# A new TensorE order and a new load order for the opening of a fused attention and feed-forward kernel

## Chip, cores, metric

One core of one Trainium2 chip. The metric is the device time of one execution in microseconds (us).

## The reference, cut

Attention with 8 global and 96 local keys and a bias that grows with the distance, then a feed-forward layer with a squared ReLU. The result is (3072, 512) in fp32.

```python
def _attn_ref(q, k, v, n_global, n_local):           # q, k, v: (4, 8, 768, 64) fp32; 8 global keys, 96 local ones
    scores = (1.0 / np.sqrt(D)) * np.matmul(q, k.transpose(0, 1, 3, 2))
    rel = pos[:, None] - pos[None, :]
    is_global = pos[None, :] < int(n_global)
    is_local = (rel >= 0) & (rel < int(n_local))
    dist = np.where(is_global & ~is_local, float(n_local), np.abs(rel))
    scores = scores + (-slopes[:, None, None] * dist[None, :, :])
    scores = np.where(is_global | is_local, scores, -1000000000.0)
    # ... cut: softmax over the last axis ...
    return np.matmul(a, v)

def _moe_ref(x, w_in, w_out):                        # x: (3072, 512), w_in: (512, 2048), w_out: (2048, 512)
    h = np.maximum(x @ w_in, 0.0)
    return h * h @ w_out
```

## The kernel before

The kernel holds q, k, v and the weights in fp16. A class `Plan` receives all work as operations with needs and estimated costs, and lists it. The order on TensorE and the order of the loads (issued by GpSimd) are given; the orders on ScalarE and VectorE, and which of the eight PSUM banks a product takes, follow from the plan's own simulation. So a new TensorE order moves VectorE's and ScalarE's work too.

For the first batch the TensorE order is one string. T2 turns q and k of tile 2 (a tile is 128 tokens; T0 turns two tiles). S2o and S2b are scores of tile 2 against its own keys and against those of the tile before. V2 is not TensorE work: VectorE copies v of tile 2 to `vb` and puts the global rows of tile 0 into it. A20 and A21 multiply by v (four heads each), X20 and X21 turn the result for the first layer, and F, G, E, D are first-layer blocks of tile 0, tiles 1 and 2, tiles 3 and 4, and tile 5. F0, G00 and G01 need quarter c0 of w_in, F1 and G10 need c1, and so on.

```python
OPENING = """T0 T2 S0o S1b A01 S1o A00 T3 S2b X01 S2o A10 A11 T4 S3b V1 X00 X11 A21 S4o A20 F1 X21 S3o
X10 S4b X20 F0 G00 V2 T5 V3 V4 G11 A30 G10 A31 S5o G30 G31 S5b A41 G01 F3 X30 G21 A40 X31 F2
X40 X41 G20 A50 E00 A51 E01 E11 X50 X51 E10 D0 D1"""
    # ... cut ...
LOADING = """v0 k2 q2 k3 v2 v1 q3 v4 k4 q4 c1 c0 q5 k5 v3 c3 v5 c2"""
```

How a name of the load string becomes a DMA, and what V and A need:

```python
        def rows(src, name, t, rank=None):
            def emit(e):
                dst = (x.bt.v[:, x.half * HT + t, :, 0:D] if name == "v"
                       else staged(x, name)[:, t, :, :])
                dma = nc.gpsimd.dma_start(out=dst, in_=src[x.b, :, r0 + t * P:r0 + (t + 1) * P, :]
                                          .rearrange("h p d -> p h d"))
                if x.hb > 3 and name == "sq" and t == 0:
                    for turn in halves[x.hb - 1].turns + halves[x.hb - 2].turns[-1:]:
                        behind(dma, turn)
                if name == "sk":
                    x.last_load = dma
            return plan.load(0.86, emit, vbefore if name == "v" else before, rank,
                             1.6 if x.hb == 0 else 2.6)
    # ... cut ...
    def load_w_in(c):
        n = d_ff // 4
        w_in_op[c] = plan.load(2.55, lambda e: nc.gpsimd.dma_start(
            out=w_in_sb[:, :, c * n:(c + 1) * n],
            in_=moe_w_in[:, c * n:(c + 1) * n].rearrange("(k p) f -> p k f", p=P)))
    # ... cut ...
    def fix_v(bt, t0, t1):
        def emit(e):
            copy(e, bt.vb[:, t0 - 1:t1 - 1], bt.v[:, t0:t1])
            copy(e, bt.vb[0:GR, t0 - 1:t1 - 1], bt.v[0:GR, 0:1].to_broadcast(
                [GR, t1 - t0, H, D + 1]))
        op = plan.add({"DVE": 0.85}, emit, [bt.v_in[0], *bt.v_in[t0:t1]],
                      wait=0.0 if bt is batches[0] else 4.0)
        for t in range(t0, t1):
            bt.vb_ops[t] = op
    # ... cut ...
        needs = st["weighs"][a0 // 2::2] + [bt.v_in[r]]
        if r > 0:
            needs.append(bt.vb_ops[r - 1] if r > 1 else bt.v_in[0])
        job = plan.pe(4 * len(kinds) * 0.035, emit, needs, 1)
    # ... cut ...
    for name in LOADING.split():
        load_jobs[name]()
    # ... cut ...
    for name in OPENING.split():
        jobs[name]()
```

Where the plan expects TensorE to stand still ahead of a product that takes a bank, and only before 24 us, it puts in products with a tile of zeros ("dummies"), to hold the clock:

```python
    def warm(ps):
        fp32 = ps.dtype == FP32
        n = min(512, ps.shape[-1]) if fp32 else P
        for _ in range(int(plan.spare / (n / 2400 + 0.003))):
            if fp32:
                nc.tensor.matmul(ps[:, 0:n], lhsT=zero[:, 0:P], rhs=zero[:, 0:n], start=True,
                                 stop=True)
            else:
                nc.tensor.transpose(out=ps[:, 0:n], in_=zero[:, 0:P], identity=ident)
```

The softmax here doesn't subtract the row's maximum and nothing guards it: scores larger than these inputs give would overflow.

## Time and profile before

| | before |
|---|---|
| time, median of 3 | 214.99 us (214.2 to 215.36) |
| time, median of 6, beside the changed kernel | 214.40 us (214.2 to 215.36) |
| span in the trace | 212.7 us |
| start of S0o, the first product after T2 | 9.95 us |
| start of D0, the last block of the opening | 37.89 us |
| from S0o to D0 | 27.94 us |

All that the change can touch lies before D0. From there both kernels run the same work with TensorE never idle, so **the start of D0 is the marker**: read it first, and ask what moved it. In the TensorE timeline it is found 0.87 us (one block of eight products) after the start of the line that ends the opening. The prediction below shows the page and the timelines of this kernel. One view it only tells of is VectorE's timeline (start, length, engine, line, operation, output and input, shape, count; in brackets idle time ahead and what ended it):

```profile
12.42 0.91 DVE L202 COPY vb<-v 128x520 f16<-128x520 f16 x2
13.25 0.16 DVE L770 RECIPROCAL rec<-av 128x4 f32<-128x4 f32 x1
```

A V is two copies of 0.7 to 0.9 us together, and each A's norm is a reciprocal and a product (0.55 from start to start). They stand in one queue: a late V makes every norm behind it late, and X needs the norm.

### The profile page before, as it was taken

The page shows a single profiled execution, that of the slowest core. Times are in us where ns is not written, and L with a number is a line of the kernel's source. Part 1 is how long each engine was busy: PE and PEld are TensorE (multiplying, and loading weights), DVE is VectorE, ACT ScalarE, POOL GpSimd, SP SyncE. Part 2 cuts the span into 40 slices and gives each one's busy share as a digit, 9 for nine tenths or more (in the row PEclk, how much of TensorE's full clock was granted, in tenths as well). Part 3 has the DMA queues.
Part 4 walks back from the last instruction along what each step waited for, and adds up shares of the span by engine and source line. Part 5 has one row for each costly group of instructions (what it writes and reads, how often), then busy time and mean ns, then how long its engine had stood idle before and what let it go on. Part 6 is the DMA issues. An engine that isn't in the chain of part 4 may idle for free.

```text
span 212.7 us, 4804 instructions
## 1 busy us (share of the span) xinstructions
PE 206.0 (97%) x1908; PEld 127.3 (60%) x1908; DVE 116.7 (55%) x334; ACT 122.0 (57%) x250; POOL 66.6 (31%) x82
## 2 busy tenths in 40 slices
PE   6799999999999999999999999999999999999994
PEld 7587889755464565456654665456644665456553
DVE  7598987443582579409770679219860777114300
ACT  6789985644741885148821994148811994237421
POOL 8994643694000940095006800094000000000000
PEclk9999999999999999999999999999999999999999
DMA  6999999999935999599976997299952100320012
GB/s 176 166 174 188 191 207 210 161 154 163 201 120 154 107 154 154 133 118 172 148 113 119 158 135 146 73 137 177 130 121 99 52 18 19 89 99 2 0 52 99
DMA packets 106343, 27.06 MB, mean 127 GB/s; under 512 B 96976, under 2 KB 103376, under 8 KB 106320
## 3 DMA queue, kind: packets, MB, share of 16 engines
q0 software_dynamic: 74944, 13.11, 80.2%
q1 hardware_dynamic: 30320, 13.11, 26.7%
q10 hardware_dynamic: 1056, 0.52, 0.8%
q8 instruction: 15, 0.25, 0.5%
q14 instruction: 8, 0.07, 0.1%
HBM read 27.26 MB, written 6.29 MB: 158 GB/s over the span
## 4 chain that ended last, share of the span: by engine, by line
PE 93%; DMA 3%; POOL 1%; DVE 1%; ACT 0%; issue 0%; POOLq 0%
PE hps L560 40%; PE yps L609 37%; PE sp L464 4%; PE av L519 4%; DMA sq<-in_q_dram 3%; PE yps L637 2%; PE sp L721 2%; PE av L760 1%; PE sp L714 1%; PE trp L669 1%; PE trx L787 1%; PE trp L411 1%; POOL v L312 0%; POOL sk L312 0%; DVE tm L772 0%; ACT qk L200 0%
## 5 line engine op out<-in xcount | busy, mean ns | idle before, releaser
L560 PE MATMUL hps<-xt,w_in_sb 128*128 128x384 f16 (+2 forms) x608 | 88.5, 301 | 0.0
L609 PE MATMUL yps<-w_out_sb,h 128*128 128x512 f16 x368 | 83.0, 379 | 0.0
L560 PEld LDWEIGHTS <-w_in_sb 128*128 128x128 f16 x608 | 53.8, 98 | 26.6
L584 ACT ACTIVATE hr<-hps 128x384 f16<-128x384 f32 (+1 forms) x106 | 54.9, 526 | 14.4 <-PE hps L560 13.3
L609 PEld LDWEIGHTS <-h 128*128 128x128 f16 x368 | 34.9, 98 | 39.0
L200 ACT COPY y<-yps 128x512 f32<-128x512 f32 (+1 forms) x25 | 14.2, 569 | 66.4 <-PE yps L609 63.8
L595 DVE TENSOR_TENSOR h<-hr 128x768 f16<-128x768 f16 (+1 forms) x70 | 35.5, 519 | 23.2 <-ACT hr L584 22.8
L312 POOL DMA_DIRECT2D sq<-in_q_dram x22 | 19.4, 889 | 66.0 <-DMA xt<-tm 64.3
L477 ACT ACTIVATE ex<-sp 128x512 f16<-128x512 f32 x66 | 35.0, 621 | 1.2 <-PE sp L464 1.2
L586 DVE TENSOR_SCALAR hr<-hps 128x384 f16<-128x384 f32 (+1 forms) x16 | 9.0, 562 | 39.4 <-PE hps L560 39.4
L312 POOL DMA_DIRECT2D v<-in_v_dram x24 | 21.7, 926 | 4.4 <-DMA w_out_sb<-in_moe_w_out_dram 3.7
L497 DVE TENSOR_TENSOR phat<-ex,mask 128x1024 f16<-128x1024 f16 (+1 forms) x36 | 20.2, 596 | 2.4 <-ACT ex L477 2.4
L312 POOL DMA_DIRECT2D sk<-in_k_dram x22 | 19.5, 901 | 5.0 <-DMA w_out_sb<-in_moe_w_out_dram 3.1
L529 DVE TENSOR_TENSOR tm<-av,rec 128x384 f16<-128x384 f32 x24 | 13.4, 557 | 0.8
L519 PEld LDWEIGHTS <-phat 128*128 128x128 f16 x240 | 9.8, 97 | 3.1
L519 PE MATMUL av<-v,phat 128*128 128x65 f16 x144 | 10.9, 193 | 0.0
L202 DVE COPY vb<-v 128x520 f16<-128x520 f16 (+1 forms) x32 | 9.9, 309 | 1.6 <-DMA v<-in_v_dram 0.9
L519 PE MATMUL av<-vb,phat 128*128 128x65 f16 x96 | 10.1, 194 | 0.0
L202 DVE COPY kb<-qk 128x96 f16<-128x96 f16 (+4 forms) x56 | 8.1, 203 | 2.0 <-ACT qk L200 2.0
L464 PEld LDWEIGHTS <-qk 64*128 64x128 f16 x168 | 6.3, 94 | 4.6 <-issue 3.7
L464 PE MATMUL sp<-qk 64*128 64x128 f16 x168 | 8.8, 218 | 0.0
L527 DVE RECIPROCAL rec<-av 128x6 f32<-128x6 f32 x24 | 4.7, 194 | 7.0 <-PE av L519 6.6
(66 smaller groups left out, 136.6 us busy)
## 6 DMA issues: line engine op xcount, KB each, us to landing
out_dram<-y SPq DMA_DIRECT2D x23, 256.0 KB, 2.2
v<-in_v_dram POOLq DMA_DIRECT2D x24, 128.0 KB, 6.5
sk<-in_k_dram POOLq DMA_DIRECT2D x22, 128.0 KB, 6.2
sq<-in_q_dram POOLq DMA_DIRECT2D x22, 128.0 KB, 5.6
w_in_sb<-in_moe_w_in_dram POOLq DMA_DIRECT2D x4, 512.0 KB, 10.1
w_out_sb<-in_moe_w_out_dram POOLq DMA_DIRECT2D x4, 512.0 KB, 14.1
y<-in_k_dram ACTq DMA_DIRECT2D x2, 256.0 KB, 4.9
y<-in_q_dram SPq DMA_DIRECT2D x2, 256.0 KB, 4.4
```

Source lines behind the costliest of these rows:

```text
L200: nc.scalar.copy(out=out, in_=in_)
L202: eng(e).tensor_copy(out=out, in_=in_)
L312: dma = nc.gpsimd.dma_start(out=dst, in_=src[x.b, :, r0 + t * P:r0 + (t + 1) * P, :] .rearrange("h p d -> p h d"))
L464: nc.tensor.matmul(sp[h][:, i, :], lhsT=lhsT, rhs=bt.qk[rows, 0, r, a, :], start=True, stop=True)
L477: nc.scalar.activation(out=st["ex"][:, h], in_=sp[h], func=AF.Exp, scale=scale)
L497: eng(e).tensor_tensor(out=x.phat[a][:, :, t0:t0 + n], op=ALU.mult, in0=st["ex"][:, :, i0:i0 + 2 * n].rearrange("p e (t b) c -> p e t (b c ...
L519: nc.tensor.matmul(av[:, h, j, :], lhsT=lhsT, rhs=rhs, start=not before, stop=before or r == 0)
L529: nc.vector.tensor_tensor(out=st["tm"].rearrange("p t e d -> p e t d"), in0=av[:, :, :, 0:D], in1=rec[:, :, :, None].to_broadcast([P, 2, H ...
L560: nc.tensor.matmul(st["ps"][:, i * n:(i + 1) * n], lhsT=w_in_sb[:, kk, m * P:(m + 1) * P], rhs=x.xt[:, kk, c0:c1], start=kk == 0, stop=kk ...
L584: nc.scalar.activation(out=o, in_=i, func=AF.Relu)
L595: eng(e).tensor_tensor(out=x.h2[:, m0:m0 + width, c0:c1], in0=hr, in1=hr, op=ALU.mult)
L609: nc.tensor.matmul(st["ps"], lhsT=x.h2[:, m, j * P:(j + 1) * P], rhs=w_out_sb[:, m, :], start=m == 0, stop=m == NFT - 1)
```

## The change

The intent: an order found by a search, which counts with eight shared banks, and with a load as done only when the last of its DMA engines has landed. Nothing else is touched.

```diff
--- before.py
+++ after.py
@@ -17,13 +17,13 @@
 
 
 
-OPENING = """T0 T2 S0o S1b A01 S1o A00 T3 S2b X01 S2o A10 A11 T4 S3b V1 X00 X11 A21 S4o A20 F1 X21 S3o
-X10 S4b X20 F0 G00 V2 T5 V3 V4 G11 A30 G10 A31 S5o G30 G31 S5b A41 G01 F3 X30 G21 A40 X31 F2
-X40 X41 G20 A50 E00 A51 E01 E11 X50 X51 E10 D0 D1"""
-
-
-
-LOADING = """v0 k2 q2 k3 v2 v1 q3 v4 k4 q4 c1 c0 q5 k5 v3 c3 v5 c2"""
+OPENING = """T0 T2 S0o S1o S2b V1 S1b A00 T3 V2 A01 S2o A10 S3o A11 A21 T4 X11 X01 S3b A20 X00 T5 X21 S4o
+X20 X10 F1 S4b A31 G11 V3 G10 G01 F0 A41 X31 A30 G00 S5b A40 F3 X30 G30 F2 X41 V4 X40 S5o
+G21 E10 E00 E11 A50 G20 A51 X50 G31 X51 E01 D0 D1"""
+
+
+
+LOADING = """v1 q2 k2 k3 q3 v0 v2 q5 q4 k4 k5 c1 v3 c0 v4 c3 c2 v5"""
```

Of the order, S1o, S2b and S1b now stand ahead of the first A, and V1 and V2 early. Of the loads, v1 goes first and v0 sixth, all of q and k ahead of the weights.

## The prediction

> **What bounds the kernel now.** I read first the page's shares and the chain that ended last, then the busy time by stretch, then the TensorE timeline of the first 46 us with its waits, and last the VectorE and ScalarE timelines there.
>
> ```profile
> PE 206.0 (97%) x1908; PEld 127.3 (60%) x1908; DVE 116.7 (55%) x334; ACT 122.0 (57%) x250; POOL 66.6 (31%) x82
> ...
> PE 93%; DMA 3%; POOL 1%; DVE 1%; ACT 0%; issue 0%; POOLq 0%
> ```
>
> TensorE is busy 206.0 of 212.7 us and holds 93% of the chain. By stretch (columns: window, length, then busy us and count of PE, PEld, DVE, ACT, POOL):
>
> ```profile
> 5.00:10.00 5.00, 3.45 (x49) 2.90 (x47) 3.31 (x7) 3.97 (x9) 5.00 (x7) 1.00 2.26 179
> ...
> 15.00:20.00 5.00, 4.56 (x96) 3.74 (x93) 4.04 (x17) 4.83 (x12) 3.10 (x4) 1.00 1.42 197
> 20.00:25.00 5.00, 5.00 (x76) 4.26 (x73) 4.58 (x14) 5.00 (x13) 2.89 (x4) 1.00 1.86 183
> ...
> 50.00:100.00 50.00, 50.00 (x452) 28.14 (x450) 28.91 (x88) 28.63 (x59) 16.00 (x19) 1.00 1.28 147
> ```
>
> From 20 to 200 us TensorE never stops, so nothing can be won there by order. The change touches only what runs before about 38 us, and the question is how early the opening's list is worked off. The marker is the first 128-column product of D0, which both lists put last: in the timeline it comes 0.87 us (one E block) after the start of the last line below, so at 37.89 us.
>
> ```profile
> 7.56 0.89 PE L216 MATMUL trp<-ident,zero 128*128 128x128 f16 x13
> 9.49 0.40 PE L669 MATMUL trp<-ident,sq 128*128 128x128 f16 x4 [1.04 <-DMA sq<-in_q_dram]
> ...
> 11.70 0.62 PE L213 MATMUL av<-zero 128*128 128x260 f16 x4
> ...
> 13.29 0.33 PE L216 MATMUL trp<-ident,zero 128*128 128x128 f16 x3
> ...
> 17.83 0.20 PE L760 MATMUL av<-vb,ph 128*128 128x65 f16 x1
> 18.42 0.40 PE L721 MATMUL sp<-qk 64*128 64x128 f16 x8 [0.40 <-ACT qk L200]
> ...
> 37.02 8.02 PE L560 MATMUL hps<-xt,w_in_sb 128*128 128x256 f16 x72
> ```
>
> T2 starts at 9.49, when its q tile lands. The products with "zero" are dummies that the kernel puts into expected waits, so they count as lost time and not as work.
>
> **How much is lost in the opening.** I add up the real work after T2's start from the distances between starts in this timeline: T 0.45 (4 of them), S with the distance products 0.87 (5), S without 0.33 and 0.10 of pause ahead of it (6), A of row 0 0.13 (2), other A 0.25 (10), X 0.11 (12), F 0.89 (4), G and E 0.87 (12). That is 1.80 + 4.35 + 2.58 + 0.26 + 2.50 + 1.32 + 3.56 + 10.44 = 26.8 us. The stretch lasts 37.89 - 9.49 = 28.4 us. So about 1.6 us are lost: 0.46 and 0.17 in dummies, some 0.7 around A21 and S4o (16.7 to 18.4 us), about 0.15 before T5 at 23.05, the rest in small pieces. **1.6 us, 0.75% of the time, is the most that a better order after T2 can win**; another 1.9 us lie before T2, from 7.56 to 9.49.
>
> **What the Trainium skill says.**
> - "DMA: Bandwidth & Descriptors", section "Why a DMA increments its semaphore by 16 and not by 1": a transfer runs on up to 16 engines and only the full 16 means that all data landed. That is the "last landing" which the search counts. The trace gives one landing per load, and it is what ends the wait: the third load, q2, is issued at 3.60 and lands 5.8 us later; T2 starts at 9.49.
> - "PSUM — Partial Sum Buffer", section "PSUM bank collisions raise a hardware error": two engines must not touch one bank at once, and a compiler serialises ScalarE against VectorE too. The trace agrees: T2's result is copied by ScalarE at 10.15 for 0.59 us and by VectorE only at 10.77. So a tile turned by both engines costs the sum of both copies.
> - "TensorE: Matmul & The Clock Gate", section "Part 1: The HAM clock gate": the clock falls after some 3.4 us of idleness, and warm 128-column products start 55.6 ns apart. Here 8 transposes take 0.45 us, 56 ns each, and the granted clock is 1.00 in every stretch. The longest gap in the new order is far shorter, so the dummies that it drops should not cost clock.
>
> **The change part by part.**
> *Dummies.* The instruction order of the built kernels has 40, 13, 4 and 3 dummies before, 40, 13 and 1 after. That takes out three wide ones at about 0.11 us and three narrow ones at 0.056: 0.5 us of TensorE time, which counts only if no wait comes in its place.
>
> *Loads.* The same 18 loads in another order. They land at a steady pace: in the order before, the issue plus the time to landing gives 7.7, 8.5, 9.45, 10.3, 11.3, 12.25, 13.0, 14.1, 15.4, 15.9 us for the ten small ones, then c1 18.3, c0 20.8, q5 21.6, k5 22.8, v3 23.8, c3 25.9, v5 26.9, c2 29.3; so about 0.95 for a small one, 2.4 for a w_in quarter. I keep the pace and deal the new names out. q2 is second (8.5), k2 third (9.45): the q half of T2 can run early and only 4 transposes remain after 9.49, so T2 ends 0.23 us earlier. v0 goes from first to sixth (7.7 to 12.25). q5 and k5 come before the weights (14.1, 16.8), c1 moves to 19.2, c0 to 22.7, c3 stays at 25.8, c2 to 28.3.
>
> *The order.* The new list does five score blocks at once after T2 (two waves of eight banks) and puts A, X and F behind. I walk it with these rows: an exp 0.49 from start to start (four take 2.06, the last 0.60), a qk copy 0.34 on VectorE or 0.49 on ScalarE, reciprocal and tm 0.55 a pair, V 0.70 to 0.83, kb 0.5, two mask products 0.75, an X copy 0.24.
>   - TensorE runs S0o S1o S2b S1b A00 T3 A01 S2o without a stop from 9.72 to 14.78. ScalarE follows with the exps: S0o at 10.7, S1b's second ends at 14.9. A10 waits for it, 0.15.
>   - VectorE is the tight one. V1 needs v0, so it starts at 12.35. In its order stand V1, V2, A00's norm, two T3 copies (both on VectorE now), A01's norm, kb, A10's and A11's norm: 0.80 + 0.70 + 0.55 + 0.68 + 0.55 + 0.5 + 0.55 + 0.55 = 4.9, plus 0.08 for the end of the last: 17.3. X11 needs A11's norm; TensorE is done with T4 at 16.75. **Stall 0.6.** A21 waits 0.15 for S2o's exps on the way.
>   - VectorE goes on: A21's norm, S3o's two mask products, X01's copy, A20's norm (19.4), kb, T5's copy (20.2), after which ScalarE copies T5's other half in the same bank, to 20.85. X20 waits about 0.1 for A20's norm, S4b waits 0.25 for T5.
>   - From S4b (20.9) on I find no further stop. G01 at 23.2 has c0 at 22.7; F0 ends at 25.0 and A41's weights are ready at 24.9; F3 at 27.2 has c3 at 25.8; F2 at 29.0 has c2 at 28.3.
>
> Losses after: 0.15 + 0.15 + 0.6 + 0.1 + 0.25, some 1.3 us, of which 0.23 is eaten from the earlier end of T2. So D0 starts at 9.49 - 0.23 + 26.8 + 1.3 = 37.4, against 37.9: **0.5 us earlier**. As TensorE is without a pause from there to the end, the 0.5 goes through whole: 214.99 - 0.5 = 214.5. Since my VectorE durations are somewhat long (V and kb were slower where GpSimd issued next to them), I lean by 0.1: 214.4 us.
>
> **The rivals.**
> 1. *The search's own hope*: all waits gone, the whole 1.6 us plus 0.2 from T2: 213.2. For it: VectorE needs only to be 0.5 faster than in my walk for X11 to start on time. Against it: VectorE would work without a pause from 12.3 to 20, which no stretch of the profile before shows (4.58 of 5 us at most).
> 2. *The chain of v0*: the move of v0 from first to sixth makes V1, V2 and all norms late, and the stall at X11 and those behind it (X20, S4b, A41) grow instead of sharing one delay. Each 0.1 us of extra VectorE time is then on the path. For it: the walk shows VectorE and ScalarE (exps and relus without a gap until 24.5) both full. That makes 215 to 215.8.
> 3. *A load lands late*: c0, c2, k4 have only 0.5 to 0.9 us of slack; two w_in quarters swapped with small ones could shift landings by 1 us. Plus 0.5 to 1: about 215.2.
> 4. *The gain is lost later*, in the phase after 45 us. The profile speaks against it: TensorE waits for nothing there, and the w_out quarters land by about 39.5 while their first use is at 44.88.
>
> **Range and chances.** Rival 1 and rival 2 lie about evenly about the estimate; the three times before span 1.2 us. 8 in 10: 213.5 to 215.3. Faster by 2% would need 4.3 us, more than all that is lost after 7.56; slower by 2% would need several new stalls or a late load of 4 us. So within 2%: 0.97, faster 0.01, slower 0.02.
>
> **What would show it right or wrong.** Right: T2's q transposes stand before 9 us and its k ones at about 9.5; the wait list of TensorE names VectorE's tm before an X block near 17 us with 0.4 to 0.8; VectorE is busy almost without a pause from 12.3 to 20; D0 begins at 37.2 to 37.6; TensorE is full from 25 us on. Wrong: a wait of TensorE on a DMA after T2 (rival 3), D0 after 37.9 (rival 2), no wait above 0.2 after 10 us and D0 by 36.5 (rival 1), or a difference in the total that D0's start does not show (rival 4).

## More of the kernel before

`V1` is two copies: the first reads only v1, the second only v0.

## The result, and the profile after

| | before | after |
|---|---|---|
| median of 6 | 214.40 us (214.2 to 215.36) | 213.82 us (213.74 to 213.89) |
| ratio | 1 | 0.9963 (95%: 0.9943 to 0.9982) |
| span in the trace | 212.7 | 212.0 |
| S0o starts | 9.95 | 9.35 |
| D0 starts | 37.89 | 37.12 |
| S0o to D0 | 27.94 | 27.77 |

A ratio here is the mean time of one kernel's fast runs over that of the other's of the same rounds, so not quite the ratio of the medians. The gain is real (the interval excludes 1) and small: 0.6 us of the median, 0.77 us at D0. Against 2% it counts as the same.

The page of the changed kernel, engine shares and the chain that ended last:

```profile
PE 206.4 (97%) x1902; PEld 127.6 (60%) x1902; DVE 116.3 (55%) x332; ACT 122.5 (58%) x252; POOL 66.5 (31%) x82
...
PE 88%; POOL 6%; DMA 5%; DVE 0%; ACT 0%; issue 0%; POOLq 0%
```

TensorE has six products fewer (the dummies). The chain looks different: GpSimd and a DMA now hold 11% instead of 4%. Its pieces in order of time (start, length, what) tell which:

```profile
9.75 1.75 POOL sk L312 x2
13.07 9.78 DMA w_in_sb<-in_moe_w_in_dram
22.90 1.94 PE hps L560 x24
```

GpSimd issues load after load without a pause until 13.07, where it issues c0; c0 lands at 22.9, and G01, its first user, starts on that. In the kernel before the same view went from q2's landing straight over into TensorE's work.

The busy time by stretch (columns as in the prediction: window, length, busy us and count of PE, PEld, DVE, ACT, POOL, then clock, DMA share, GB/s):

```profile
5.00:10.00 5.00, 4.60 (x60) 4.32 (x59) 3.47 (x6) 4.42 (x10) 5.00 (x7) 1.00 2.26 179
...
15.00:20.00 5.00, 4.73 (x90) 3.68 (x87) 4.61 (x19) 4.64 (x11) 3.46 (x5) 1.00 1.50 196
20.00:25.00 5.00, 4.90 (x73) 4.16 (x71) 4.48 (x15) 4.68 (x11) 2.33 (x4) 1.00 1.47 198
```

TensorE is busy 1.15 us longer ahead of 10 and 0.17 longer between 15 and 20, and 0.10 shorter between 20 and 25, where it was full before. Busy is not the same as won: about 0.5 of the 1.15 us is T0, whose 16 transposes started 107 ns apart in this trace (5.89 to 7.60) and about 60 in the other, with waits between them. The granted clock reads 1.00 in both and doesn't show this. T0 ends close to 7.6 us in both and T2's k half waits for a load after it, so nothing is lost or won by it. The TensorE timeline at the places that the prediction named:

```profile
8.32 0.39 PE L669 MATMUL trp<-ident,sq 128*128 128x128 f16 x4
9.11 0.40 PE L669 MATMUL trp<-ident,sk 128*128 128x128 f16 x4 [0.40 <-DMA sk<-in_k_dram]
9.35 0.61 PE L714 MATMUL sp<-dmask,slope_id 128*128 128x128 f16 x8
...
16.42 0.40 PE L669 MATMUL trp<-ident,sk 128*128 128x128 f16 x4
16.86 0.40 PE L787 MATMUL trx<-ident,tm 128*128 128x128 f16 x4
...
36.25 8.02 PE L560 MATMUL hps<-xt,w_in_sb 128*128 128x256 f16 x72
```

T2 runs in two halves, at 8.32 and 9.11. X11 starts at 16.86. D0 follows the last line by 0.87, at 37.12.

Short waits are hidden in this timeline, because the ends of pipelined products are modelled and overlap the next ones. The waits of the weight loads show them. The wait list of PEld from 9 to 40 us (total, times, longest):

```profile
PEld L669 <- DMA sk<-in_k_dram: 0.8, 2, 0.6
PEld L787 <- DVE tm L772: 0.5, 2, 0.3
PEld L560 <- DMA w_in_sb<-in_moe_w_in_dram: 0.4, 1, 0.4
```

In words: T2 and T4 wait for their k tiles, X11 and X20 for VectorE's `tm`, and G01 for c0:

```profile
22.89 1.77 PEld L560 LDWEIGHTS <-w_in_sb 128*128 128x128 f16 x24 [0.38 <-DMA w_in_sb<-in_moe_w_in_dram]
```

VectorE's timeline, to set beside the lines of before:

```profile
10.90 0.72 DVE L202 COPY vb<-v 128x520 f16<-128x520 f16 x1
11.98 0.39 DVE L202 COPY vb<-v 32x520 f16<-32x520 f16 x1 [0.35 <-DMA v<-in_v_dram]
12.94 0.63 DVE L202 COPY vb<-v 128x520 f16<-128x520 f16 x2 [0.58 <-DMA v<-in_v_dram]
13.50 0.16 DVE L770 RECIPROCAL rec<-av 128x4 f32<-128x4 f32 x1
```

V1's big copy runs at 10.90, long before v0 lands; only its small second copy waits for v0. V2 waits for v2 and is done just ahead of the first norm.

### The profile page after: what moved, and what is told of

It is laid out like the page before. It is cut to its first block, busy times and chain, and to the rows that moved or that the text cites. A ratio compares the mean times of both kernels' runs of the same rounds, so it can differ in the third digit from the quotient of the medians.

```text
span 212.0 us, 4795 instructions
## 1 busy us (share of the span) xinstructions
PE 206.4 (97%) x1902; PEld 127.6 (60%) x1902; DVE 116.3 (55%) x332; ACT 122.5 (58%) x252; POOL 66.5 (31%) x82
## 4 chain that ended last, share of the span: by engine, by line
PE 88%; POOL 6%; DMA 5%; DVE 0%; ACT 0%; issue 0%; POOLq 0%
PE hps L560 39%; PE yps L609 38%; DMA w_in_sb<-in_moe_w_in_dram 5%; PE sp L464 4%; PE av L519 4%; POOL v L312 2%; POOL sk L312 2%; POOL sq L312 2%; PE yps L637 2%; PE trp L411 1%; PE av L760 1%; POOL w_in_sb L369 0%; PE trx L787 0%; PE sp L721 0%; DVE ident L239 0%; ACT y L200 0%
## 5 line engine op out<-in xcount | busy, mean ns | idle before, releaser
L586 DVE TENSOR_SCALAR hr<-hps 128x384 f16<-128x384 f32 x15 | 8.3, 554 | 38.7 <-PE hps L560 38.7
```

## The experiments

The theory after the trace, called A in the texts: the opening is set by whatever wait ends last, and that is c0's landing or VectorE's queue; a shift at D0 passes whole into the time. B is the rival that each text names. Times stand beside runs of the kernel before in the same rounds on the same chip. Edits are to the changed kernel unless it says otherwise.

### 1. The loads alone

```diff
-LOADING = """v0 k2 q2 k3 v2 v1 q3 v4 k4 q4 c1 c0 q5 k5 v3 c3 v5 c2"""     (order of the kernel before kept)
+LOADING = """v1 q2 k2 k3 q3 v0 v2 q5 q4 k4 k5 c1 v3 c0 v4 c3 c2 v5"""
```

> The order of before with the new order of loads. Theory A (order and loads only work together): F0 in the old order stands at 21.15 us and now needs c0, which lands at 22.9 in the trace of after instead of 20.8; TensorE waits about 1.7 us there, the wait of T5 (0.14) goes, everything behind F0 follows unchanged, so D0 starts about 39.5 instead of 37.9 and the time is about 216.0 us, 0.7% above before. Theory B (the gain comes from the loads, because T2's q half runs early): at or below 213.9.

Measured: 216.0 us beside 214.38, ratio 1.0075 (1.0062 to 1.0088). **The new loads alone cost 1.6 us.** The old order asks for c0 early, with F0; it lands later now, and the plan filled the wait with dummies. TensorE's timeline:

```profile
21.64 1.03 PE L213 MATMUL hps<-zero 128*128 128x512 f16 x4
22.78 1.39 PE L560 MATMUL hps<-xt,w_in_sb 128*128 128x128 f16 x19
```

F0 stands at 22.78, 1.6 us behind the 21.15 of the kernel before. D0 starts at 39.39, 1.5 later.

### 2. The order alone

```diff
-OPENING = """T0 T2 S0o S1b A01 S1o A00 T3 S2b X01 ...        (loads of the kernel before kept)
+OPENING = """T0 T2 S0o S1o S2b V1 S1b A00 T3 V2 A01 ...
```

> The order of after with the old order of loads. Theory A (order and loads only work together): T5 stands at 17.9 us in the new order and k5 lands at 22.8 in the old order of loads, so TensorE stops for 4 to 5 us at T5, of which the 0.3 at c0 and some small waits come back: about 218 us, 1.7% above before. Theory B (the gain comes from the TensorE order, with fewer dummies): at or below 213.9.

Measured: 217.88 us beside 214.38, ratio 1.0164 (1.015 to 1.0178). **The new order alone costs 3.5 us.** It asks for T5 early, and the old loads bring q5 and k5 behind two quarters of weights:

```profile
18.81 3.79 PE L216 MATMUL trp<-ident,zero 128*128 128x128 f16 x65
22.44 0.39 PE L669 MATMUL trp<-ident,sq 128*128 128x128 f16 x4
```

The 65 dummies fill 3.6 us in front of T5. So neither half carries the gain: each alone loses more than both together win.

### 3. c0 later by one load

```diff
-... c1 v3 c0 v4 c3 c2 v5
+... c1 v3 v4 c0 c3 c2 v5
```

> After, with the load of v4 put ahead of c0. Theory A (the landing of c0 at 22.9 us is what the end hangs on in after, all earlier waits being slack): c0 lands one small load later, 0.9 us, and the time rises by 0.8 to 0.9, to about 214.7 us. Theory B (the VectorE chain from v0 binds, as my prediction had it, with c0 0.5 us ahead of its need): 0.4 or less.

Measured: 214.37 us beside 214.38, ratio 0.9997 (0.9985 to 1.001); the changed kernel's was 0.9963.

```profile
23.61 1.10 PE L560 MATMUL hps<-xt,w_in_sb 128*128 128x256 f16 x9 [0.76 <-DMA w_in_sb<-in_moe_w_in_dram]
...
36.95 1.26 PE L560 MATMUL hps<-xt,w_in_sb 128*128 128x256 f16 x12
```

c0 lands at 23.57 instead of 22.85. G01 starts 0.72 us later than in the changed kernel, D0 0.70 later (37.82, 0.87 after the last line), the median 0.55. From c0's first use to D0 it is 14.21 us here (37.82 - 23.61) and 14.23 there (37.12 - 22.89). A delay of c0 passes through whole: **c0's landing is on the path**, with no slack. The time itself lies between the numbers of the two theories and would not decide between them; the equal shifts of G01 and D0 do.

### 4. k4 earlier

```diff
-... v2 q5 q4 k4 k5 c1 ...
+... v2 q4 k4 q5 k5 c1 ...
```

> After, with q4 k4 loaded ahead of q5 k5; the same instructions on TensorE. T4's wait for k4 (about 0.25 us at 16.2) should vanish. Theory A (c0 binds): no change of the time, within 0.1 us of 213.8, while the wait at G01 for c0 grows by what T4 saves. Theory B (the waits from 15 to 20 us are on the path): 0.2 us less.

Measured: 213.8 us beside 214.38, ratio 0.9974 (0.996 to 0.9987): no change. T4 no longer waits for k4, but X11 starts where it did:

```profile
16.09 0.39 PE L669 MATMUL trp<-ident,sk 128*128 128x128 f16 x4
16.84 0.40 PE L787 MATMUL trx<-ident,tm 128*128 128x128 f16 x4 [0.36 <-DVE tm L772]
```

The wait for k4 turned into a longer wait for `tm`. Up to X11, VectorE's queue is the limit, and the two waits lay beside each other. A's number came, but not its detail: the wait at G01 did not grow (its weight loads waited 0.25 us, against 0.38 in the changed kernel).

### 5. The kernel before without its late dummies

```diff
     def warm(ps):
+        plan.warmed = getattr(plan, "warmed", 0) + 1      (the kernel before)
+        if plan.warmed > 2:
+            return
```

> Before, without the seven dummy products after T2 (four wide ones ahead of A01, three narrow ones ahead of T3). Theory A: they stand in waits that stay (A01 waits for ScalarE's exps, T3 for the landing of q3), so taking them out gives at most 0.15 us: 214.3. Theory B (dropping dummies is TensorE time won, 0.63 us, and explains the gain of after): 213.8.

Measured: 214.44 us beside 214.44, ratio 0.9999 (0.9987 to 1.0012). The time is A's, but its reason is not what the trace shows. S0o starts at 9.99, 0.04 later than before, yet S4o 0.24 earlier (18.18 instead of 18.42), and T5 0.23 earlier. Then TensorE's weight loads for G30 wait for c3:

```profile
18.18 0.40 PE L724 MATMUL sp<-qk 64*128 64x128 f16 x8 [0.16 <-ACT qk L200]
26.10 1.64 PEld L563 LDWEIGHTS <-w_in_sb 128*128 128x128 f16 x16 [0.29 <-DMA w_in_sb<-in_moe_w_in_dram]
```

(The first line is from TensorE's timeline, the second from that of its weight loads.) c3 lands at 26.06; in the kernel before, TensorE came to G30 at 26.16. So some 0.28 of the dummies' 0.63 us was TensorE time in the way, and leaving them out won it as far as G30, where the old order of loads took all but 0.06 back. Leaving them out costs no clock: T5's products still start 55 ns apart. Whether the six that the change drops are a part of its gain, this run can't say.

### 6. A30 ahead of G01, to cover the wait for c0

```diff
-... V3 G10 G01 F0 A41 X31 A30 G00 ...
+... V3 G10 A30 G01 F0 A41 X31 G00 ...
```

> After, with A30 moved from behind X31 to ahead of G01, the first user of c0. Theory A (c0's landing at 22.8 to 22.9 us is what the end hangs on): the wait of 0.27 us at G01 is filled with A30's 0.25 us of work, all behind G01 is shorter by that, 213.6 us. Theory B (the path runs elsewhere, the wait at G01 is only its shadow): no change, 213.8.

Measured: 213.88 us beside 214.44, ratio 0.997 (0.9958 to 0.9983): the same as the changed kernel, where A had expected a gain. G01 does not wait for c0 any more, but G10 ends at 22.97 instead of about 22.64, so with A30's 0.25 TensorE comes to G01 at 23.21. The reason stands on VectorE:

```profile
12.94 1.08 DVE L200 COPY vb<-v 128x520 f16<-128x520 f16 x2 [0.56 <-DMA v<-in_v_dram]
13.95 0.16 DVE L768 RECIPROCAL rec<-av 128x4 f32<-128x4 f32 x1
```

V2's two copies took 1.08 us against 0.63 in the changed kernel (about 0.85 in runs 3 and 4), so the first norm came 0.45 us later and X11 stood at 17.19. The wait was not removed; VectorE's queue had become the limit.

### 7. T2's loads first, with A30 ahead

```diff
-LOADING = """v1 q2 k2 k3 q3 v0 v2 q5 q4 k4 k5 c1 v3 c0 v4 c3 c2 v5"""     (and the edit of 6)
+LOADING = """q2 k2 k3 q3 v0 v2 v1 q4 k4 q5 k5 c1 v3 c0 v4 c3 c2 v5"""
```

> As the run with A30 ahead, and the loads in the order q2 k2 k3 q3 v0 v2 v1 q4 k4 q5 k5, then as in after: k2 lands at about 8.1 instead of 9.1, so T2 and what follows it starts about 0.8 us earlier, and v0 and v2 land a place earlier. c0 keeps its place. Theory A (c0 caps): the time is that of the run with A30 ahead, within 0.1 us, and the wait at G01 grows to 0.5 us or more. Theory B (the start at T2 and the VectorE chain are the path): 0.5 us or more below it, about 213.1.

Measured: 213.95 us beside 214.44, ratio 0.9976 (0.9963 to 0.9988): no gain. T2 is done earlier (its second half starts at 8.84), but the plan put two dummies behind it and S0o starts at 9.50. And v1 is now seventh, so both V come late and in one piece:

```profile
12.09 1.83 DVE L200 COPY vb<-v 128x520 f16<-128x520 f16 x4 [0.85 <-DMA v<-in_v_dram]
```

The first norm follows at 13.85, and X11 stands at 17.24. A had the time right, but not the reason: it saw c0, and the limiter was VectorE's queue.

### 8. An order and loads of my own search

```diff
-OPENING = """T0 T2 S0o S1o S2b V1 S1b A00 T3 V2 ...       (and warm as in 5)
+OPENING = """T0 T2 S0o S2b S2o V1 A00 S1b X00 A01 V2 S1o T3 A21 S3b ...
-LOADING = """v1 q2 k2 k3 q3 v0 v2 q5 q4 k4 k5 c1 v3 c0 v4 c3 c2 v5"""
+LOADING = """k2 q2 v0 v1 q3 k3 v2 q4 k4 k5 q5 c1 c0 v3 v4 c3 c2 v5"""
```

> An order of TensorE and loads of my own, with T2's loads first and c0 ahead of v3, v4 (so c0 lands about 21.9), no dummies after T2. If the loads of the weights and the start at T2 are what binds, freeing both gives 0.4 to 0.8 us below after, 213.0 to 213.4. If the waits of VectorE and ScalarE take over (the order was chosen with rough durations), it gives nothing or loses: 213.8 or more.

Measured: 216.26 us beside 214.44, ratio 1.008 (1.0067 to 1.0094): slower. The order was chosen with rough durations. TensorE's wait list from 9 to 40 us:

```profile
PE trx L790 <- DVE tm L775: 1.7, 3, 1.1
PE av L763 <- ACT ph L737: 0.8, 2, 0.6
PE sp L724 <- DVE qk L202: 0.7, 2, 0.4
```

That is 3.2 us of waits for VectorE and ScalarE. A search over an order is worth what its durations are worth.

### 9. V2 held back

If VectorE's queue ahead of X11 is the limit, take V2 out of it. V2 was held until behind A21's norm, and `warm` was cut as in 5:

```diff
     op = plan.add({"DVE": 0.85}, emit, [bt.v_in[0], *bt.v_in[t0:t1]],
-                  wait=0.0 if bt is batches[0] else 4.0)
+                  wait=(5.0 if t0 == 2 else 0.0) if bt is batches[0] else 4.0)
```

> After, with V2 (two VectorE copies, 0.63 to 1.08 us in the traces so far, first needed by A31) held back behind A21's norm, so that A00's to A11's norms come that much earlier; no dummies after T2. Theory A (two limits of nearly the same length: c0's landing at 22.85 us and the VectorE chain through V2): X11 starts before 16.75 us, but G01 then waits longer for c0, and the time stays at 213.7 to 213.8. Theory B (the VectorE chain alone binds): 213.4 or less.

Measured: 214.43 us beside 214.43, ratio 0.9995 (0.9982 to 1.0009): the whole gain lost. Both theories missed. VectorE's timeline:

```profile
13.16 0.18 DVE L771 RECIPROCAL rec<-av 128x4 f32<-128x4 f32 x1 [0.67 <-PE av L761]
...
17.50 1.00 DVE L200 COPY vb<-v 128x520 f16<-128x520 f16 x2
```

and TensorE's at X20:

```profile
20.04 0.40 PE L788 MATMUL trx<-ident,tm 128*128 128x128 f16 x4 [0.94 <-DVE tm L773]
```

Without V2, VectorE idles 0.67 us ahead of the first norm. V2's full microsecond stands at 17.50 instead, ahead of S3o's masks and A20's norm, and X20 waits 0.94 us. The first norm comes 0.34 us sooner than in the changed kernel (13.16 against 13.50), but X11 does not (16.84 against 16.86), because T4 still waits for k4, until 16.61. VectorE's norm after X11 stands at 17.16 against 17.18, so up to there V2 had cost the changed kernel nothing. **VectorE is a queue of work and not one late wait**: what is moved out of one place is paid at the next.

### 10 and 11. The same with A30 ahead, and with k4 early too

```diff
+ the edit of 6, on that of 9                (10)
+ the edits of 6 and 4, on that of 9         (11)
```

> As the run with V2 held back, and A30 ahead of G01. Theory A (two limits; the run with A30 ahead alone gained nothing because V2 took 1.08 us there): now both are eased, and 0.25 us is won, 213.5 to 213.6; c2's landing at 28.4 is the next limit and lets no more through. Theory B (c0's wait is no limit): as the run with V2 held back.

> As the run before, with q4 k4 ahead of q5 k5 in the loads, so that T4 doesn't wait for k4. Theory A: no more than that run, within 0.1 us, as c0 and c2 stay where they are; theory B (the stretch from 15 to 18 us is on the path): 0.2 us less.

Measured: 214.34 us (0.9993, 0.9979 to 1.0007) and 214.16 us (0.9983, 0.9969 to 0.9997), beside 214.43. The first loses nearly all of the gain, the second about half of it. The second's six times fall into two groups, 213.86 to 214.0 and 214.31 to 214.49; its trace is from the slower one, and what divides them is not known. X20 waits 0.95 and 0.91 us again. S0o starts at 9.21 in the first and at 9.55 in the second, yet D0 at 37.65 and 37.69. That is no clean test of an early start, since k4 moved too: the chain that ended last goes back to k4's landing at 16.41 in the first, and to k2's at 9.27 in the second.

### 12. The v tiles ahead, with A30 ahead

Here V1 and V2 are to be done before the first norm needs VectorE.

```diff
-LOADING = """v1 q2 k2 k3 q3 v0 v2 q5 q4 k4 k5 c1 v3 c0 v4 c3 c2 v5"""     (and the edit of 6)
+LOADING = """v1 q2 k2 v0 v2 k3 q3 q4 k4 q5 k5 c1 v3 c0 v4 c3 c2 v5"""
-                  wait=0.0 if bt is batches[0] else 4.0)
+                  wait=(1.2 if t0 == 1 else 0.0) if bt is batches[0] else 4.0)
```

> As the run with A30 ahead, but V2 taken off the VectorE chain without putting it on another stretch: v0 and v2 are loaded ahead of k3 and q3, k4 ahead of q5, and VectorE does V1 and V2 before A00's norm is ready (13.2 us) instead of after. Theory A (two limits, VectorE's queue of work up to 20 us and c0's landing at 22.85): X11 starts by 16.7 us instead of 16.86 to 17.2, TensorE reaches G01 with A30 done at about 22.6 to 22.8 and waits for c0 up to 0.3 us; the time is 213.5 to 213.6, 0.25 us below after, and no lower, as c0 and c2 stay. Theory B (something behind G01 binds): 213.8.

Measured: 213.7 us (213.46 to 213.77) beside 214.49, ratio 0.9959 (0.9946 to 0.9972), not to be told from the changed kernel's 0.9963. VectorE:

```profile
12.56 1.01 DVE L200 COPY vb<-v 128x520 f16<-128x520 f16 x2
13.49 0.16 DVE L768 RECIPROCAL rec<-av 128x4 f32<-128x4 f32 x1
```

V2 is early, but takes 1.01 us, and the first norm stands at 13.49, as in the changed kernel (13.50). G01 starts at 22.97 without a wait. Then F2 finds the next landing, that of c2:

```profile
28.69 0.90 PEld L558 LDWEIGHTS <-w_in_sb 128*128 128x128 f16 x16 [0.29 <-DMA w_in_sb<-in_moe_w_in_dram]
```

D0 starts at 37.12, to the hundredth where it does in the changed kernel.

### The runs side by side

| run | S0o | D0 | S0o to D0 | median beside before | wait that the trace shows as the limit |
|---|---|---|---|---|---|
| before | 9.95 | 37.89 | 27.94 | | S4o for ScalarE's `qk` |
| after | 9.35 | 37.12 | 27.77 | -0.58 | G01 for c0 |
| 1 | 9.46 | 39.39 | 29.93 | +1.62 | F0 for c0 |
| 3 | 9.29 | 37.82 | 28.53 | -0.01 | G01 for c0 |
| 4 | 9.26 | 37.06 | 27.80 | -0.58 | X11 for `tm`, then G01 for c0 |
| 5 | 9.99 | 37.83 | 27.84 | 0.00 | G30 for c3 |
| 6 | 9.43 | 37.17 | 27.74 | -0.56 | X11 for `tm` |
| 7 | 9.50 | 37.21 | 27.71 | -0.49 | X11 for `tm` |
| 9 | 9.30 | 37.79 | 28.49 | 0.00 | X20 for `tm` |
| 12 | 9.39 | 37.12 | 27.73 | -0.79 | F2 for c2 |

D0 tells the time within 0.25 us in each row (columns 3 and 5, against before). Five kernels (after, 4, 6, 7, 12) end within 0.15 us of each other at D0, by three different waits. No version clearly beats the changed kernel. Runs 2, 8, 10 and 11 are left out of the table; their times stand above.

## Why the prediction was right, point by point

- **The bound was right.** Only the time before D0 moved, and it passed through: 0.77 us at D0, 0.7 in the span, 0.6 in the median. From 25 us on TensorE is full. The search's own hope (213.2, all waits gone) and the slow rivals (about 215 and more) were not what came; the estimate of 214.4 was 0.6 too high, because it started from the median of three runs, 214.99, and the six runs give 214.40. The gain itself, estimated at 0.5 (0.6 with the lean), was 0.58 in the medians.
- **Its own signs came only in part.** T2's q half ran before 9 us, and TensorE was full from 25 us on. D0 at 37.12 fell just outside 37.2 to 37.6, the waits for `tm` before X11 and X20 were 0.3 at most and not 0.4 to 0.8, and VectorE still idled 0.58 us ahead of V2. One sign of "wrong" came too, TensorE's waits for loads after T2 (k4, c0), though not the 0.5 to 1 us that rival 3 gave them.
- **T2's two halves were right in kind.** The q half ran before 9 us, at 8.32. The k half came at 9.11 and not at 9.5, since the third load landed about 0.35 us sooner than the pace of before had it. With the same first three loads, T2's k half started between 8.97 and 9.32 in nine kernels' traces; with the old first three, T2 started at 9.15 to 9.54 in three. So this difference is of the size of the spread, and I cannot say that the order of the loads made it.
- **How much of the gain is S0o's earlier start is not shown.** It is 0.60 us earlier, the time from S0o to D0 only 0.17 shorter; the prediction had 0.23 and 0.3, so that its sum came near is in part luck. Against booking 0.60 to T2: in the changed kernel D0 is pinned by c0's landing (run 3), and the chain leads from there to GpSimd's issues and not to T2. For it: in the five kernels that end alike the time from S0o to D0 is 27.71 to 27.80 us, while S0o starts anywhere from 9.26 to 9.50. No run moved k2's landing alone with the rest of the changed kernel kept.
- **The stall of X11 was mis-sized.** I had 0.6 us, the trace shows about 0.2. The step that failed is "V1 needs v0, so it starts at 12.35": only V1's small second copy needs v0, and the big one ran at 10.90. V2 then started at 12.94, when v2 landed, and not at 13.15, and took 0.63 instead of 0.70, so the first norm came at 13.50 and not at 13.85. X11 came at 16.86 and not at about 17.3. Of the other small waits, those at A10, A21 and X20 are there, with about 0.15, 0.15 and 0.2; the 0.25 of S4b is not (0.10, the usual pause). A slip that cost nothing: the new list puts four score blocks at once after T2, not five; the walk itself has them right.
- **"From S4b on I find no further stop" was wrong.** G01 waits for c0, some 0.3 us. I had c0 at 22.7 and G01 at 23.2; c0 landed at 22.9, and TensorE, earlier by X11's 0.5, came at about 22.6. The slack was eaten from both sides, more from the early one: a stall removed upstream arrives at the next landing as a wait. Rival 3 named c0 and k4, and k4 did stop T4 for about 0.25, but neither cost what rival 3 feared: T4's wait lay beside the one for VectorE (run 4), and the one at G01 was only as long as TensorE came early.
- **The dummies were right as far as tested.** The prediction let their 0.5 us count only if no wait came in its place. In run 5 leaving them out of the kernel before won 0.28 up to G30, and a wait for c3 came in its place; no clock was lost. What they are worth within the change was not tested.
- **The sum.** I had losses of 1.3 us after S0o; 27.77 less the 26.35 us of real work from S0o on (26.8 less T2's 0.45) leaves 1.42. So the total was close, with less at X11 and S4b and more at T4 and G01: errors that cancelled.

What stays open: why the first loads land up to 0.35 us earlier or later from kernel to kernel with the same order, and why the two copies of V2 take 0.63 us in one trace and 1.08 in another that gives VectorE the same work there. GpSimd was issuing loads beside them in both. The Trainium skill, "GPSIMD Engine Reference", section "1. Specifications", says that GpSimd shares its SBUF interfaces with VectorE and contends with some of its instructions; that could be it, but no run here separates it. Open too is how the 0.6 us divides among the earlier start, the dropped dummies and the order after S0o.

## What to carry to other kernels

An order of work and an order of loads are one thing: here each half of the change alone lost 1.6 and 3.5 us, and both together won 0.6. When several chains have almost the same length (a queue on VectorE, the landing of c0, the landing of c2), easing one gains only the distance to the next, so work out that distance before working on the wait. And put a wait off the path or on it by moving it (as c0 by one load) and reading a marker further down, not by its length.

## What the Trainium skill lacked or had wrong

- "DMA: Bandwidth & Descriptors", section "Anatomy of one DMA — SWDGE (gpsimd) path", gives about 2.0 us fixed plus the bytes at 436 GB/s for one transfer; the estimate from that is 2.3 us for a load of 128 KB (2.6 us if the 256 KB of fp32 that it reads are counted). Here the first such load took 5.5 to 6.0 us from issue to landing, with the four first-tile loads running beside it, and c0 (512 KB), issued with six loads ahead of it that had not landed, 9.78 us. So the formula does not carry over to a load among others in flight, and that section has no figure for one; the trace's pace, about 0.95 us a small load and 2.4 a quarter of w_in, served here.
